# Splitting the second expert's weight quarters at other tiles of a retention and mixture-of-experts kernel

## The chip, the cores and the metric

The kernel runs on one core of one Trainium2 chip. The metric is the device time of one execution in microseconds (us). Three executions of the kernel before were timed; their median is 397.33 us (395.97 to 397.36).

## What is computed

A retention layer (linear attention with a decay per head) gives 3072 rows of 512 numbers. Each row then goes through one of 8 experts, two matrix products with a ReLU between them, and is scaled by its gate weight.

```python
# q, k, v: (4, 8, 768, 64); w_gate (512, 8); w1 (8, 512, 1024); w2 (8, 1024, 512)
for t in range(S):
    state = gamma * state + einsum('bhd,bhe->bhde', k[:, :, t], v[:, :, t])
    y[:, :, t] = scale * einsum('bhd,bhde->bhe', q[:, :, t], state)
x = y.transpose(0, 2, 1, 3).reshape(B * S, H * D)
logits = x @ w_gate
expert_idx = argmax(logits, axis=1)
gate_w = softmax(logits)[arange(N), expert_idx]
for e in range(E):
    mask = expert_idx == e
    out[mask] = gate_w[mask, None] * (maximum(x[mask] @ w1[e], 0) @ w2[e])
```

## The kernel before

The first part (to some 117 us of the span) computes the retention, the gates and the place of each row, and scatters the rows into a region of device memory for each expert. The second part, `moe_main`, goes through the experts in the order e = 0 to 7, one after the other; the change lies in it alone. Expert 0's rows come in two groups. The first group's first layer runs at the end of the first part, so that `moe_main` begins with the second group: 224 rows, from 121.5 us on.

**Precision.** Every matrix product is made of three: each operand is split into a high part (a rounded copy) and a low part (the rest), and TensorE multiplies high by high, low by high and high by low. So every weight and every activation passes through a split: a copy on ScalarE (ACT) that makes the high part, then a subtraction on VectorE (DVE) that makes the low part.

**Weights.** An expert's weights are four quarters of 1 MB. Quarters 0 and 1 belong to the first layer (tiles 0 to 3 and 4 to 7), quarters 2 and 3 to the second. "Quarter 2/0" below is quarter 0 of expert 2. `fetch` (L139) is a DMA from SyncE's queue (SP) into one of two buffers, `raw`; so a quarter's fetch waits until the quarter two before it in the order of fetches has been split. `split` (L142) splits one half of a quarter: an ACT copy (L147, `whi<-raw`) and a DVE subtraction (L148, `wlo<-raw,whi`).

**An expert's steps.** The first layer has 8 tiles f (`for f in range(KF)`). In each, TensorE makes 12 matmuls into one of three PSUM tiles `ph` (L959), ACT the ReLU `hh` (L971), and DVE the low part `hl` (L973); TensorE may write a `ph` again when the `hl` of three tiles before has been made. The second layer has steps k: four of 24 matmuls for experts 1 to 6 (L1000), two for expert 0 (L998; its third step is behind a count that leaves it out here). A step's 24 matmuls take `hh` and `hl` of tile 0 first and of tile 7 last. The results lie in two PSUM tiles `py` in turn; DVE takes them out with `yo` (L886, expert 0) or a transposition `Z` (L896), and step k + 2 needs that `py` free.

**Rows of the next expert.** `fetch_x` clears 96 rows behind the region (L702, from `zero`) and then loads the rows with four DMAs on SP (L186, `xgs<-xs_dram`); the loads wait until the clearing has landed. `prep_x` prepares up to 128 rows: a DVE transposition (L736, `xt`), an ACT copy (L745, `xh`) and the low part (L746, `xl`, on DVE or GpSimd). The first matmul of the next expert needs `xh` of all its pieces.

**What sets the order.** The order on each engine is the order of the code. `job(f, fn, ...)` files a call into a list for place f; places 0 to 7 stand behind the ReLU and low part of tile f, place `KF + k` behind step k. In each place the calls run in the order in which they were filed. Every engine takes its instructions strictly in that order, and SP its DMAs.

Of the kernel before, what the change touches and what calls it, by code (L numbers as in the profile page):

```python
# [37 lines left out]
KF = F // P  # L38
# [74 lines left out]
def retention_moe(ctx, tc, qkv, wts, cst, gdec, out):  # L113
# [587 lines left out]
    def clear_behind(e, zero):  # L701
        nc.sync.dma_start(out=x_rows[bass.ds(end_at[e], ZROWS), :], in_=zero)  # L702

    natural = {0: (sidx0, meta0)}
    moe_main(tc, wparts, fetch, split, xhl1, hidden_early, third, lim, xgs, clear_behind, load_x, load_meta, token_index, regions, beyond, limit, spare, natural,
             overflow, out)
    most = nc.values_load(top[0:1, 0:1], min_val=0, max_val=N)  # L707
# [93 lines left out]
def moe_main(ctx, tc, wparts, fetch, split, xhl1, hidden_early, third, lim, xgs, clear_behind, load_x, load_meta, token_index, regions, beyond, limit, spare, natural,  # L801
             overflow, out):
    nc = tc.nc
    sidx0, meta0 = natural[0]
# [101 lines left out]
    with tc.manual_schedule():  # L906
        for e in range(E):
# [9 lines left out]
            job = lambda f, fn, *a: jobs[f].append((fn, a))  # L917
            if e == 0:
                job(2, nc.gpsimd.memset, zero, 0.0)
                job(3, nc.vector.memset, rare[0:widths[0][2]], 0.0)  # L920
                job(4, token_index, sidx0[:, 1:4], meta0[:, 1:4], lim[:, 1:4], "joint")
                for i in range(3):
                    job(1 + i // 2, nc.vector.memset, phs[i][:, CAPS[1] - 3 * STEPS[1]:], 0.0)
                for j in range(nxt):
                    job(6 + j // 2, prep_x, 1, j, nc.vector if j % 2 else nc.gpsimd)
            if e == 1:
                job(1, put_rows, 0, rare, 2)
                job(3, overflow)
# [5 lines left out]
                job(0, fetch_x, e + 1)  # L934
            if e > 0:
                for i, eng in halves:
                    job(i, split, e, 3, i, eng)
            if back:
                nb = blocks[e - 1]
                for j in range(nb):  # L940
# [1 line left out]
                    job(at, weigh, e - 1, j, 1)  # L942
                    job(at, put_slices, e - 1, j)
            if more:
                for part, s0, f0 in ((0, 3, 0), (1, 6, 2)) if e else ((0, 2, 4), (1, 5, 7)):
                    job(f0, fetch, e + 1, part if e else part + 2)
                    for i, eng in halves:
                        job(s0 + i, split, e + 1, part, i, eng)
                if e:
                    job(6, fetch, e + 1, 2)  # L950
# [27 lines left out]
            for k in range(steps):  # L978
# [40 lines left out]
                    turn(e, py, k)  # L1019
                if more and k < 2:  # L1020
                    for i, eng in halves:
                        if i == k:
                            split(e + 1, 2, i, eng)
                if more and e and k == 0:
                    fetch(e + 1, 3)
# [143 lines left out]
```

## Time and profile before

| | before |
|---|---|
| median of three executions | 397.33 us |
| the profiled execution, device time | 395.59 us |
| its span, first to last instruction | 393.6 us |
| TensorE busy | 380.0 us, 97% |
| VectorE busy | 258.0 us, 66% |
| ScalarE busy | 154.3 us, 39% |
| GpSimd busy | 163.1 us, 41% |
| granted TensorE clock, mean | 0.995 |

The span is one profiled execution; the device time lies 2.0 us above it. Since TensorE is busy nearly throughout, what counts is where it stands still, and what it waits for there. A time in the trace is counted in us from the span's start.

### The profile page before, as it was taken

What the parts mean: (1) busy time and instruction counts of PE and PEld (TensorE: products, weight loads), DVE (VectorE), ACT (ScalarE), POOL (GpSimd) and SP (SyncE); (2) the same over time, 40 slices, a digit from 0 to 9 for tenths busy, and PEclk for the clock granted to TensorE, in tenths of its full rate; (3) what the DMA queues carried; (4) which work ended last, traced back from release to release, by engine and by line L of the source; (5) the groups of instructions that cost most, each with busy time, mean ns of one, the idle gap of its engine ahead of it and who ended that gap; (6) DMA issues with size and microseconds to landing.
All of it is one profiled execution on the core that took longest, in us unless ns stands there. A gap on an engine that the chain in (4) does not pass through costs nothing. (4 is left out here: it accounts for less than half of the span.)

```text
span 393.6 us, 8661 instructions
## 1 busy us (share of the span) xinstructions
PE 380.0 (97%) x3255; PEld 353.6 (90%) x3255; DVE 258.0 (66%) x563; ACT 154.3 (39%) x316; POOL 163.1 (41%) x153
## 2 busy tenths in 40 slices
PE   7999999998899989999999999999999999999994
PEld 4888888896799869999999999999999999999973
DVE  4547758786586787774785677477747857776330
ACT  2335444551473534633442354054334515523100
POOL 0322656846551032000653174328316614831652
PEclk9999999999899999999999999999999999999999
DMA  7998799995457659483568175835754783530111
GB/s 273 415 380 335 287 414 422 402 359 184 142 193 205 155 169 301 151 205 122 149 239 194 52 245 171 210 113 158 210 151 147 259 209 103 188 120 11 55 29 69
DMA packets 30190, 80.65 MB, mean 205 GB/s; under 512 B 4795, under 2 KB 18751, under 8 KB 23716
## 3 DMA queue, kind: packets, MB, share of 16 engines
q1 hardware_dynamic: 24868, 66.87, 52.6%
q0 software_dynamic: 5248, 12.69, 9.0%
q8 instruction: 58, 0.95, 1.0%
q14 instruction: 16, 0.13, 0.1%
HBM read 65.07 MB, written 15.19 MB: 204 GB/s over the span
## 5 line engine op out<-in xcount | busy, mean ns | idle before, releaser
L726 POOL DMA_INDIRECT out<-Z,sidx x82 | 93.9, 1145 | 134.1 <-DVE Z L901 107.8
L148 DVE TENSOR_TENSOR wlo<-raw,whi 128x1024 fp32r<-128x1024 f32 (+1 forms) x67 | 75.6, 1131 | 11.0 <-ACT whi L147 9.4
L147 ACT CAST whi<-raw 128x1024 fp32r<-128x1024 f32 (+1 forms) x72 | 67.6, 952 | 5.8 <-PE ph L959 2.9
L971 ACT ACTIVATE hh<-ph 128x64 fp32r<-128x64 f32 (+7 forms) x72 | 32.3, 460 | 90.6 <-PE ph L959 79.5
L1000 PE MATMUL py<-hl,whi 128*128 128x392 f32 (+4 forms) x192 | 66.1, 344 | 0.0
L1000 PE MATMUL py<-hh,whi 128*128 128x392 f32 (+4 forms) x192 | 66.1, 344 | 0.0
L1000 PE MATMUL py<-hh,wlo 128*128 128x392 f32 (+4 forms) x192 | 66.0, 344 | 0.0
L973 DVE SCALAR_TENSOR_TENSOR hl<-ph,hh 128x64 fp32r<-128x64 f32 (+7 forms) x72 | 36.4, 515 | 35.7 <-ACT hh L971 33.5
L959 PE MATMUL ph<-xh,whi 128*128 128x392 f32 (+5 forms) x224 | 49.3, 342 | 0.0
L959 PE MATMUL ph<-xh,wlo 128*128 128x392 f32 (+5 forms) x224 | 49.0, 340 | 0.0
L959 PE MATMUL ph<-xl,whi 128*128 128x392 f32 (+5 forms) x224 | 48.9, 340 | 0.0
L959 PEld LDWEIGHTS ph<-xh,whi 128*128 128x128 f32 x224 | 40.3, 188 | 0.5
L959 PEld LDWEIGHTS ph<-xh,wlo 128*128 128x128 f32 x224 | 40.4, 188 | 0.2
L959 PEld LDWEIGHTS ph<-xl,whi 128*128 128x128 f32 x224 | 40.2, 188 | 0.2
L745 ACT CAST xh<-xt 128x512 fp32r<-128x512 f32 (+7 forms) x27 | 14.8, 552 | 58.5 <-DVE xt L736 58.5
L1000 PEld LDWEIGHTS py<-hl,whi 128*128 128x128 f32 x192 | 36.2, 188 | 0.3
L1000 PEld LDWEIGHTS py<-hh,wlo 128*128 128x128 f32 x192 | 36.1, 188 | 0.2
L1000 PEld LDWEIGHTS py<-hh,whi 128*128 128x128 f32 x192 | 36.1, 188 | 0.2
L248 POOL TENSOR_TENSOR vs<-qkv_t,cs 128x512 f32<-128x512 f32 x19 | 19.8, 1044 | 36.1 <-DMA qkv_t<-qkv 34.2
L262 DVE TENSOR_TENSOR Sb<-sp,xgs 128x512 f32<-128x512 f32 x48 | 29.9, 682 | 7.4 <-PE sp L259 4.8
L726 POOL DMA_INDIRECT xs_dram<-xn,KEY x24 | 25.2, 1052 | 16.6 <-issue 5.3
L278 ACT ACTIVATE ub<-U,cs 128x64 f32<-128x64 f32 x80 | 18.5, 314 | 28.6 <-PE U L273 25.6
(161 smaller groups left out, 519.7 us busy)
## 6 DMA issues: line engine op xcount, KB each, us to landing
raw<-w SPq DMA_DIRECT2D x32, 1024.0 KB
qkv_t<-qkv SPq DMA_DIRECT2D x18, 1024.0 KB
qkv_t<-qkv SPq DMA_DIRECT2D x4, 768.0 KB
xgs<-xs_dram SPq DMA_DIRECT2D x12, 211.2 KB
qkv_t<-qkv SPq DMA_DIRECT2D x4, 512.0 KB
xgs<-xs_dram SPq DMA_DIRECT2D x8, 227.5 KB
out<-Z,sidx POOLq DMA_INDIRECT x82
xs_dram<-zero SPq DMA_DIRECT2D x6, 195.0 KB
```

The source lines that it names most:

```text
L147: nc.scalar.copy(out=hi[:, h], in_=raw[:, h])
L148: engine.tensor_tensor(out=lo[:, h], in0=raw[:, h], in1=hi[:, h].bitcast(F32), op=ALU.subtract)
L248: engine.tensor_tensor(out=vs, in0=qs[g][:, 2].rearrange("a (h d) -> a h d", d=D), in1=cv[:, c, :].unsqueeze(2).broadcast_to([P, H, D]), o ...
L262: nc.vector.tensor_tensor(out=Sb[:, r], in0=sps[r], in1=M[:, r], op=ALU.mult)
L278: nc.scalar.activation(out=ubs[g % 3][:, p], in_=U[:, p], func=AF.Copy, scale=k_("ratio")[:, at:at + 1])
L726: sc = tc.nc.gpsimd.indirect_dma_start(out=out, out_offset=bass.IndirectOffsetOnAxis(ap=index, axis=0), in_=rows, in_offset=None, bounds_c ...
L745: nc.scalar.copy(out=xh[:, :, sl], in_=src)
L959: nc.tensor.matmul(out=ph[:, :w], lhsT=wparts[e, f // 4][a][:, kd, fo:fo + P], rhs=x[:, kd, :w], start=(n == 0), stop=(n == 3 * KD - 1))
L971: nc.scalar.activation(out=to, in_=of, func=AF.Relu)
L973: nc.vector.scalar_tensor_tensor(out=low, in0=of, scalar=0.0, in1=to.bitcast(F32), op0=ALU.max, op1=ALU.subtract)
L1000: nc.tensor.matmul(out=py[:, :cols], lhsT=a[:, f % 4, k * P:(k + 1) * P], rhs=x[:, :cols], **se)
```

## The change

Four edits in the tables of jobs of `moe_main`; nothing is added to or taken from the computation.

- Quarter 1/0 is split in expert 0's tiles 3 and 4 (tiles 2 and 3 before). Quarter 1/1 is split in the places of the second layer's steps 0 and 1 (tiles 5 and 6 before). Quarter 1/2 is split in expert 1's tiles 0 and 1 (steps 0 and 1 of expert 0 before), quarter 1/3 in its tiles 2 and 3 (tiles 0 and 1 before).
- In expert 1, quarter 2/0 is split in tiles 5 and 6 (3 and 4 before) and quarter 2/1 in the places of steps 0 and 1 (tiles 6 and 7 before), behind quarter 2/2, which stays there. From expert 2 on nothing moves.
- The pieces of expert 1's rows are prepared in tiles 6, 6, 7 and step 0 (6, 6, 7, 7 before).
- The token index of expert 0 is made one tile earlier.

```diff
-                job(4, token_index, sidx0[:, 1:4], meta0[:, 1:4], lim[:, 1:4], "joint")
+                job(3, token_index, sidx0[:, 1:4], meta0[:, 1:4], lim[:, 1:4], "joint")
...
-                    job(6 + j // 2, prep_x, 1, j, nc.vector if j % 2 else nc.gpsimd)
+                    job((6, 6, 7, KF)[j], prep_x, 1, j, nc.vector if j % 2 else nc.gpsimd)
...
                 for i, eng in halves:
-                    job(i, split, e, 3, i, eng)
+                    if e == 1:
+                        job(i, split, e, 2, i, eng)
+                    job(i + 2 * (e == 1), split, e, 3, i, eng)
...
-                for part, s0, f0 in ((0, 3, 0), (1, 6, 2)) if e else ((0, 2, 4), (1, 5, 7)):
+                for part, s0, f0 in ((0, 3 + 2 * (e == 1), 0), (1, 6 + 2 * (e == 1), 2)) if e else ((0, 3, 4), (1, KF, 7)):
                     job(f0, fetch, e + 1, part if e else part + 2)
                     for i, eng in halves:
                         job(s0 + i, split, e + 1, part, i, eng)
...
                     for i, eng in halves:
-                        if i == k:
+                        if e and i == k:
                             split(e + 1, 2, i, eng)
```

In the rows below, `wlo` is the low part of a half quarter, and its `raw` buffer tells the quarter.

VectorE in expert 0, before, from tile 5's split to tile 6 (`raw_1873` is quarter 1/1):

```order
L148 TENSOR_TENSOR wlo_2303<-raw_1873,whi_2302 128x1024
L973 SCALAR_TENSOR_TENSOR hl0_1660<-ph0_2147,hh0_1659 128x64
L973 SCALAR_TENSOR_TENSOR hl_2319<-ph0_2147,hh_2318 128x160
L736 STREAM_TRANSPOSE xt_2326<-xgs_71 128x4x4x32
L736 STREAM_TRANSPOSE xt_2330<-xgs_71 128x4x4x32
L746 TENSOR_TENSOR xl_2325<-xt_2330,xh_2324 128x4x128
```

and now, from tile 6 to step 0:

```order
L975 SCALAR_TENSOR_TENSOR hl0_1660<-ph0_2147,hh0_1659 128x64
L975 SCALAR_TENSOR_TENSOR hl_2315<-ph0_2147,hh_2314 128x160
L736 STREAM_TRANSPOSE xt_2322<-xgs_71 128x4x4x32
L736 STREAM_TRANSPOSE xt_2326<-xgs_71 128x4x4x32
L746 TENSOR_TENSOR xl_2321<-xt_2326,xh_2320 128x4x128
L975 SCALAR_TENSOR_TENSOR hl0_1660<-ph1_2148,hh0_1659 128x64
L975 SCALAR_TENSOR_TENSOR hl_2343<-ph1_2148,hh_2342 128x160
L736 STREAM_TRANSPOSE xt_2348<-xgs_71 128x4x4x32
L886 TENSOR_SCALAR yo_2378<-py0_2144,meta0_84 128x4x4x32
L736 STREAM_TRANSPOSE xt_2383<-xgs_71 128x2x4x32
L746 TENSOR_TENSOR xl_2321<-xt_2383,xh_2320 128x4x56
L148 TENSOR_TENSOR wlo_2388<-raw_1873,whi_2387 128x1024
```

Quarter 1/1 has moved from ahead of tile 6 to behind the take-out of step 0 (`yo`), and the last piece of the rows with it.

SP's queue around the end of expert 0, before (`raw_2282` and `raw_2362` are quarters 1/2 and 1/3, the branches of L1005 and L842 mark the last step of expert 0 and the first tile of expert 1):

```order
L139 DMA raw_2282<-w 128x2048
L139 DMA raw_2362<-w 128x2048
L702 ISA
L702 DMA xs_dram_61<-zero_2154 96x520
L1005 UNCONDITIONAL_BRANCH
L842 UNCONDITIONAL_BRANCH x3
```

and now (`raw_2280` and `raw_2352`):

```order
L139 DMA raw_2280<-w 128x2048
L1007 UNCONDITIONAL_BRANCH
L842 UNCONDITIONAL_BRANCH x3
L139 DMA raw_2352<-w 128x2048
L842 UNCONDITIONAL_BRANCH
L702 ISA
L702 DMA xs_dram_61<-zero_2154 96x520
```

The order of the DMAs is the same; the fetch of quarter 1/3 now waits for a split that stands at the very end of expert 0, and the clearing and expert 2's row loads stand behind it.

VectorE in expert 1, steps 0 and 1, before (`raw_2888` is quarter 2/2):

```order
L736 STREAM_TRANSPOSE xt_2949<-xgs_71 128x4x4x32
L746 TENSOR_TENSOR xl_2948<-xt_2949,xh_2947 128x4x128
L896 STREAM_TRANSPOSE Z_3052<-py0_2144 128x14x32
L148 TENSOR_TENSOR wlo_3055<-raw_2888,whi_3054 128x1024
L842 UNCONDITIONAL_BRANCH
L736 STREAM_TRANSPOSE xt_3060<-xgs_71 128x4x4x32
L746 TENSOR_TENSOR xl_2948<-xt_3060,xh_2947 128x4x128
L896 STREAM_TRANSPOSE Z_3052<-py1_2145 128x14x32
```

and now (`raw_2884` is quarter 2/2, `raw_2638` quarter 2/1):

```order
L736 STREAM_TRANSPOSE xt_2943<-xgs_71 128x4x4x32
L842 UNCONDITIONAL_BRANCH x2
L746 TENSOR_TENSOR xl_2942<-xt_2943,xh_2941 128x4x128
L896 STREAM_TRANSPOSE Z_3046<-py0_2144 128x14x32
L148 TENSOR_TENSOR wlo_3049<-raw_2884,whi_3048 128x1024
L842 UNCONDITIONAL_BRANCH
L148 TENSOR_TENSOR wlo_3055<-raw_2638,whi_3054 128x1024
L736 STREAM_TRANSPOSE xt_3058<-xgs_71 128x4x4x32
L746 TENSOR_TENSOR xl_2942<-xt_3058,xh_2941 128x4x128
L896 STREAM_TRANSPOSE Z_3046<-py1_2145 128x14x32
```

Between the take-outs of steps 0 and 1 there are now two low parts instead of one.

## Rows read from the trace of the kernel before

**Rows 1.** The page, engines: busy us (share of the span) and instructions.

```profile
PE 380.0 (97%) x3255; PEld 353.6 (90%) x3255; DVE 258.0 (66%) x563; ACT 154.3 (39%) x316; POOL 163.1 (41%) x153
```

**Rows 2.** Timeline, TensorE: start, duration, instruction, count [idle before and its releaser].

```profile
131.60 0.70 PE L959 MATMUL ph<-xhl,whi 128*128 128x224 f32 x4 [0.35 <-DVE hl L973]
...
133.04 0.41 PE L998 MATMUL py<-whi,hh 128*128 128x512 f32 x1
...
137.59 0.39 PE L998 MATMUL py<-whi,hl 128*128 128x512 f32 x1
138.45 0.50 PE L998 MATMUL py<-whi,hh 128*128 128x512 f32 x1 [0.48 <-ACT hh L971]
...
140.00 0.50 PE L998 MATMUL py<-whi,hl 128*128 128x512 f32 x1 [0.81 <-DVE hl L973]
...
145.97 0.93 PE L959 MATMUL ph<-xh,whi 128*128 128x392 f32 x4
...
163.08 0.34 PE L1000 MATMUL py<-hh,whi 128*128 128x392 f32 x1
...
180.25 0.92 PE L959 MATMUL ph<-xh,whi 128*128 128x422 f32 x4
```

**Rows 3.** Timeline, ScalarE.

```profile
132.79 1.05 ACT L147 CAST whi<-raw 128x1024 fp32r<-128x1024 f32 x1 [2.42 <-PE ph L959]
...
138.19 0.41 ACT L971 ACTIVATE hh<-ph 128x64 fp32r<-128x64 f32 x2
...
157.68 1.05 ACT L147 CAST whi<-raw 128x1024 fp32r<-128x1024 f32 x1 [2.39 <-DMA raw<-w]
...
167.37 1.05 ACT L147 CAST whi<-raw 128x1024 fp32r<-128x1024 f32 x1
...
177.30 0.42 ACT L745 CAST xh<-xt 128x272 fp32r<-128x272 f32 x1 [2.40 <-DVE xt L736]
```

**Rows 4.** Timeline, VectorE.

```profile
146.78 1.22 DVE L148 TENSOR_TENSOR wlo<-raw,whi 128x1024 fp32r<-128x1024 f32 x1
...
161.56 1.13 DVE L973 SCALAR_TENSOR_TENSOR hl<-ph,hh 128x440 fp32r<-128x440 f32 x2
...
168.50 1.19 DVE L148 TENSOR_TENSOR wlo<-raw,whi 128x1024 fp32r<-128x1024 f32 x1
...
171.00 0.69 DVE L746 TENSOR_TENSOR xl<-xt,xh 128x512 fp32r<-128x512 f32 x1 [0.69 <-ACT xh L745]
...
176.16 0.65 DVE L896 STREAM_TRANSPOSE Z<-py 128x448 f32<-128x448 f32 x1 [0.53 <-PE py L1000]
```

**Rows 5.** Timeline, SP: the issue of DMAs (the duration is that of issuing).

```profile
133.85 0.35 SPq L139 DMA_DIRECT2D raw<-w  x1
139.83 0.35 SPq L139 DMA_DIRECT2D raw<-w  x1
...
145.95 2.00 SPq L186 DMA_DIRECT2D xgs<-xs_dram  x4
...
153.54 0.35 SPq L139 DMA_DIRECT2D raw<-w  x1
161.67 0.34 SPq L139 DMA_DIRECT2D raw<-w  x1
166.04 0.33 SPq L139 DMA_DIRECT2D raw<-w  x1
...
171.95 1.90 SPq L186 DMA_DIRECT2D xgs<-xs_dram  x4
```

**Rows 6.** Stretches: length, busy of each engine, granted clock, DMA share, GB/s.

```profile
134.75:138.25 3.50, 3.23 (x15) 2.34 (x13) 2.81 (x6) 2.13 (x4) 1.29 (x1) 1.00 0.86 302
172.75:178.25 5.50, 5.50 (x32) 5.50 (x32) 3.75 (x6) 1.04 (x2) 0.00 (x0) 1.00 1.14 198
178.25:180.75 2.50, 2.50 (x16) 2.49 (x15) 0.30 (x1) 0.00 (x0) 0.00 (x0) 1.00 0.90 357
180.75:182.00 1.25, 1.25 (x9) 1.22 (x8) 0.34 (x1) 0.00 (x0) 0.00 (x0) 1.00 0.04 7
```

## The prediction

> **What bounds the kernel now.** First the page: TensorE is busy for 380.0 us of the span and VectorE for 66% of it [rows 1], so a change of order can only win where TensorE stands still, and lose where it makes it stand still. Then TensorE's own timeline through experts 0 and 1, where everything moved lies. The reader is to see three gaps in expert 0 and none in expert 1 [rows 2]. Tile 7 waits 0.35 us for the `hl` of tile 4. Step 0 waits 0.48 us for the `hh` of tile 7 and 0.81 us for its `hl`. ScalarE's timeline shows why: the copy of quarter 1/1 waited 2.42 us until 132.79 for TensorE, and the ReLU of tile 7 came only at 138.19 [rows 3], four microseconds after step 0 had begun at 133.04. It stood behind the late copy, the ReLU of tile 6, two pieces of rows and a second copy.
>
> From 145.97 (expert 1's first tile) to 163.08 (its second layer) and 180.25 (expert 2) TensorE has no wait [rows 2]. The one wait there is ScalarE's: it stood 2.39 us until quarter 2/0 had landed at 157.68 [rows 3]. That quarter is behind expert 2's row loads in SP's queue. This stretch is full, and the change puts more into it.
>
> **Part 1: expert 0.** Twenty matmuls of step 0 take 133.04 to 137.59, 0.2275 us each [rows 2]. Two steps of 24 would take 10.9 us and the short third step 0.1; from 133.04 to 145.97 it took 12.93. So 1.9 us are lost in the steps, and some 0.4 at tile 7: 2.3 us. With the change no split stands between tile 4 and step 0. Tile 7's ReLU stands behind the copies of two row pieces, which start after tile 6 and two transpositions of some 0.7 us, and so is done near 135, 2 us before step 0 needs it. The last piece of rows comes after the take-out of step 0, some 4 us before expert 1's first tile. The token index (four small operations of a tile earlier) lies beside matmuls; its cover is the wait for the ReLU, and without it the index would cost its own 0.6 us at most. The fetch of quarter 1/2 stands behind value loads in SP and goes out at 133.85 either way [rows 5]. I count the whole gap as gone: **-2.3 us**, expert 1 begins at 143.7. Its bounds are 0 and -2.3, since no more is lost there.
>
> **Part 2: when quarter 2/0 lands.** Quarter 1/3 may be fetched when quarter 1/1 is split. The second half of that split now stands behind the take-out of step 1. In the profile the same place on VectorE held a half that began at 146.78 and took 1.22 [rows 4], so ended 2.0 us after expert 1's first matmul: now 145.7, where the fetch went out at 139.83 before. Behind it in SP stand the clearing and expert 2's row loads. From such a fetch to the row loads it took 6.1 us in one place (139.83 to 145.95) and 5.9 in the other (166.04 to 171.95) [rows 5]. So the row loads go at 151.7, and quarter 2/0 behind them.
>
> How long after the loads it lands has two rows. Expert 3's loads began at 171.95 with one quarter behind them. The engines moved 198 GB/s until 178.25, then 357 (the quarter), and were quiet after 180.75 [rows 6]: 8.8 us. Expert 2's loads began at 145.95 and quarter 2/0 was there at 157.68 [rows 3, 5], 11.7 us, with quarter 2/1 issued behind it at 153.54. The new case is the same quarter, with its follower 3 us closer. Neither row fits in every respect, so I take the middle, 10.25: it lands at **161.9** (160.5 to 163.4).
>
> The Trainium skill (DMA: Bandwidth & Descriptors, Queues, rings and completion order) says that an engine takes the descriptors of one issuing engine's ring in order. By that alone the quarter would land right behind the loads, at 160.5, and the sum below would be +0.9 instead of +2.2. The rate of 198 and then 357 GB/s agrees with the order; the 11.7 us do not agree with a landing right behind. The same section says that a completion comes only when the last of the DMA engines has reported, which leaves room for them.
>
> **Part 3: what waits for it in expert 1.** Expert 1's second layer begins 17.1 us after its first tile [rows 2], now at 160.8. ScalarE's queue is now: copy of 2/0, ReLU of tile 6, copy, ReLU of tile 7; VectorE's follows in the same manner. In the profile the same sequence, two tiles earlier, ran from the landing at 157.68 to the `hl` that started at 161.56 [rows 3, 4]; the first of its two ended about 4.4 us after the landing. So the `hl` of tile 7 is ready at 166.3. Step 0 reaches it with its last matmul, 23 x 0.179 us (17.17 us for 96 matmuls, from 163.08 to 180.25 [rows 2]) after its start: 164.9. **TensorE waits 1.4 us** (0 to 2.9). Before, the same lateness stood at tiles 3 and 4, where three `ph` tiles hid it.
>
> Quarter 2/2 takes the buffer of 2/0. Its fetch went out 4.0 us after the landing (161.67 after 157.68 [rows 3, 5]): 165.9. Landing takes 4.4 us when nothing is ahead (issued at 133.85, moved by 138.25 [rows 5, 6]) and at most 5.7 (161.67 to its copy at 167.37 [rows 3, 5]). I take 4.7, near the lower row since that one is free of other waits: 170.6. From there VectorE's queue decides: copy 1.05, `wlo` of 2/2, `wlo` of 2/1 (1.15 each at their pitch), a row piece, and only then the `Z` of step 1, on which step 3 waits for its `py`. From a `wlo` at 168.50 to the end of the next `xl` (171.00 and 0.69) it took 3.2 us [rows 4]. So `Z` of step 1 ends at 170.6 + 1.1 + 1.15 + 3.2 + 0.65 = 176.7. Step 3 would begin at 160.8 + 1.4 + 3 x 4.29 = 175.1. **TensorE waits 1.6 us.** Then two more low parts, a row piece (1.15 + 3.2) and `Z` of step 2 and the last piece (176.16 to 177.30 + 0.42 [rows 3, 4], 1.6 us) must pass, 5.8 with their overlaps, before the first matmul of expert 2 has its `xh`: 182.5. Step 3 ends at 181.0. **TensorE waits 1.5 us.** In the profile that place had no wait and expert 2 began at 180.25.
>
> The three waits make 4.5 us, less the 2.3: **+2.2 us**. The ends are landings at 160.5 with 4.4 and at 163.4 with 5.7: expert 2 at 180.8 or at 185.0, +0.5 or +4.8.
>
> **Part 4: behind.** Quarter 2/3 is fetched when 2/1 is split, some 2.3 us after that `Z`, at 179.0; expert 3's loads follow 6.0 us later and quarter 3/0 lands at 193.8 to 196.7. A tile of expert 2 takes 2.14 x 422 / 392 = 2.30 us, so its tile 7 begins at 198.6 and needs an `hl` that ends some 2.8 us after the landing, at 196.6 to 199.5. I take 0; at most 0.9. From there on the orders are the same, and a delay stays a delay. The moves of 1/2 and 1/3 into tiles 0 to 3 put one half per tile of 2.14 us on ScalarE (1.05) and VectorE (1.22), beside ReLU and `hl`; `hl` may come three tiles late, so I cost it at nothing.
>
> **Sum.** 393.6 + 2.2 = 395.8 of span, 397.8 with the 2.0 around it; the profiled execution lies 1.74 below the median. On the median: 397.33 + 2.2 = **399.5 us**.
>
> **Rivals.**
> A. Slower by more: quarter 2/0 lands as the nearest row has it, 11.7 us after the loads, and expert 2 still meets a late 3/0. 163.4 + 4.0 + 4.7 + 11.9 puts expert 2 at 184.0, +3.75, and 0.5 in its tile 7: 401.6 us. For it: the very same quarter took that long. Against: 8.8 elsewhere.
> B. Faster: the quarter does not wait for the row loads to move but shares the engines with them and lands 4.4 us after an issue near 153.9, at 158.3. Then neither tile 7 nor step 3 is late by much, expert 2 begins at 178.9 and the time is 396.0; with a landing by 157.2 all of the 2.3 stays, 395.0. It decides at a landing of 159.6, from which on expert 2 is late against 180.25. Against: the 198 GB/s while the loads move, half of what a quarter reaches [rows 6].
> C. The change doesn't do what it says in expert 0: the ReLU of tile 7 is late still, now behind the row copies. Then 1 us of step 0's gap, say, remains, and parts 2 and 3, whose times all count from the end of expert 0, come on top of it: 400.5. Against: a margin of 2 us.
>
> **How the numbers follow.** A measurement of this kernel can tell about 0.5%, 2.0 us, from no change. My forecast has a chance of 0.65; its own range is +0.5 to +3.4, and I put 0.34 above 2.0 us and 0.31 below. A has 0.16, all slower. B has 0.12: 0.07 faster by over 0.5%, 0.05 within. C has 0.04, slower. The remaining 0.03 lies within. Slower 0.54, same 0.39, faster 0.07. The range of 8 in 10 runs from 397.2 to 402.0: it leaves out B and the far end of A.
>
> **What would show it.** After the change: no wait of TensorE for `hh` or `hl` in expert 0 and expert 1's first matmul near 143.7 (part 1). The row loads near 151.7 and a wait of ScalarE for quarter 2/0 until about 162 (part 2). Waits of TensorE at the end of step 0, before step 3 and before expert 2's first matmul, for `hl`, `Z` and `xh` (part 3). If quarter 2/0 is there before 159.6, I am wrong in sign; if the three waits are there but expert 2 begins before 181, only the size is off.

## The result, and the profile after

| | kernel before | kernel after |
|---|---|---|
| median of the runs made side by side, us | 396.69 (395.97 to 397.36, 4 runs) | 401.87 (401.38 to 402.15, 4 runs) |
| span of the profiled execution, us | 393.6 | 400.0 |
| first tile of expert 0 behind the early half, us | 121.55 | 121.68 |
| expert 1 begins | 145.97 | 143.73 |
| copy of quarter 2/0 begins on ScalarE | 157.68 | 165.43 |
| expert 2 begins | 180.25 | 186.18 |
| expert 3 begins | 217.25 | 223.31 |

The ratio is 1.0129 with an interval of [1.0103, 1.0156]: the kernel after is 1.3% slower, 5.2 us. The forecast was 399.5 us, 2.2 us more than before; its range of 397.2 to 402.0 holds the time, near the upper end. That is partly luck: the kernel before came out at 396.69 this time and not at the 397.33 of the forecast, and 5.2 us on top of 397.33 would have been 402.5, outside the range.

On the page, the busy time of TensorE has grown by 4.5 us though no matmul was added, which is the first hint of a slower clock [rows 1]:

```profile
PE 384.5 (96%) x3255; PEld 355.3 (89%) x3255; DVE 258.0 (64%) x563; ACT 154.3 (39%) x316; POOL 163.0 (41%) x153
```

TensorE's timeline after (start, duration, instruction, count, idle before and its releaser), to be laid beside [rows 2]:

```profile
121.68 0.68 PE L961 MATMUL ph<-xhl,whi 128*128 128x224 f32 x4 [0.97 <-DVE xhl L680]
...
143.73 0.57 PE L961 MATMUL ph<-xh,whi 128*128 128x392 f32 x2
...
160.85 0.34 PE L1002 MATMUL py<-hh,whi 128*128 128x392 f32 x1
...
166.97 0.70 PE L1002 MATMUL py<-hh,whi 128*128 128x392 f32 x1 [2.73 <-ACT hh L973]
...
168.31 0.69 PE L1002 MATMUL py<-hl,whi 128*128 128x392 f32 x1 [0.33 <-DVE hl L975]
...
169.97 0.70 PE L1002 MATMUL py<-hl,whi 128*128 128x392 f32 x1 [0.31 <-DVE hl L975]
...
186.18 1.04 PE L961 MATMUL ph<-xh,whi 128*128 128x422 f32 x4 [1.05 <-ACT xh L745]
...
223.31 0.91 PE L961 MATMUL ph<-xh,whi 128*128 128x418 f32 x4
```

The reader sees two things. The gap in expert 0 is gone: from its first tile to expert 1 it is 22.05 us where it was 24.42. And expert 1, which had no wait before, now has four. From its first matmul to expert 2 it takes 42.45 us, where it took 34.28. Behind that nothing changes: from expert 2 to expert 3 it is 37.13 us after and 37.00 before.

SP's timeline after (the duration is that of issuing), against [rows 5]: quarter 1/3, the clearing, expert 2's row loads, then quarters 2/0 and 2/1 together, and 2/2.

```profile
145.78 0.35 SPq L139 DMA_DIRECT2D raw<-w  x1
146.47 0.37 SPq L702 DMA_DIRECT2D xs_dram<-zero  x1
154.15 2.94 SPq L186 DMA_DIRECT2D xgs<-xs_dram  x4
157.34 0.95 SPq L139 DMA_DIRECT2D raw<-w  x2
169.42 0.34 SPq L139 DMA_DIRECT2D raw<-w  x1
```

ScalarE's and VectorE's timelines after, against [rows 3, 4]: the copies of quarters 2/0 and 2/2, and VectorE's chain from the late quarter to the last row piece of expert 2.

```profile
165.43 1.04 ACT L147 CAST whi<-raw 128x1024 fp32r<-128x1024 f32 x1 [8.11 <-DMA raw<-w]
174.41 2.00 ACT L147 CAST whi<-raw 128x1024 fp32r<-128x1024 f32 x2 [3.22 <-DMA raw<-w]
```

```profile
166.51 1.22 DVE L148 TENSOR_TENSOR wlo<-raw,whi 128x1024 fp32r<-128x1024 f32 x1 [8.54 <-ACT whi L147]
167.65 0.61 DVE L975 SCALAR_TENSOR_TENSOR hl<-ph,hh 128x440 fp32r<-128x440 f32 x1
168.18 1.21 DVE L148 TENSOR_TENSOR wlo<-raw,whi 128x1024 fp32r<-128x1024 f32 x1
169.31 0.61 DVE L975 SCALAR_TENSOR_TENSOR hl<-ph,hh 128x440 fp32r<-128x440 f32 x1
...
175.49 2.36 DVE L148 TENSOR_TENSOR wlo<-raw,whi 128x1024 fp32r<-128x1024 f32 x2 [3.02 <-ACT whi L147]
...
179.77 0.64 DVE L896 STREAM_TRANSPOSE Z<-py 128x448 f32<-128x448 f32 x1
180.34 2.32 DVE L148 TENSOR_TENSOR wlo<-raw,whi 128x1024 fp32r<-128x1024 f32 x2
...
186.16 0.44 DVE L746 TENSOR_TENSOR xl<-xt,xh 128x272 fp32r<-128x272 f32 x1 [0.48 <-ACT xh L745]
```

From the copy at 165.43 every step of VectorE follows the one before it or the next landing, down to the last row piece, beside which expert 2 starts. Call the start of that copy **L**: expert 2 begins at L + 20.75.

The stretches of core 0 after show where the wait's second effect lies (length, busy time of PE, PEld, DVE, ACT and POOL, granted clock, DMA share, GB/s):

```profile
152.00:154.00 2.00, 2.00 (x13) 2.00 (x12) 1.47 (x5) 2.00 (x3) 0.03 (x1) 1.00 0.04 6
157.00:162.00 5.00, 5.00 (x30) 5.00 (x29) 0.85 (x2) 0.32 (x1) 0.00 (x0) 1.00 1.20 222
162.00:165.40 3.40, 2.23 (x13) 1.91 (x11) 0.00 (x0) 0.00 (x0) 0.00 (x0) 1.00 1.00 412
167.00:173.00 6.00, 5.33 (x13) 3.88 (x14) 4.79 (x7) 1.91 (x3) 0.00 (x0) 0.50 0.42 138
173.00:186.00 13.00, 12.12 (x67) 11.79 (x65) 8.81 (x11) 5.44 (x7) 0.00 (x0) 0.98 0.31 102
```

Behind the wait of 2.73 us the granted clock is 0.50, the 1.2 GHz level, until about 173.5; matmuls of 392 columns then follow each other at 0.33 us instead of 0.18. From 160.85 the 17.17 us of work in expert 1's second layer [rows 2] and the 3.37 us of waits would end at 181.4, and TensorE is done at 185.1, 3.7 us later. The half clock is at most 3.4 us of that, half of the 6.8 us that it lasts; what the rest is, the rows do not tell.

The first of these stretches is the second thing that was not foreseen. The row loads wait for the clearing, which landed only at 154.15, 7.7 us after its issue, though the engines moved almost nothing from 152 on.

### The profile page after: what moved, and what is told of

Read it like the earlier page. It is cut to its first block, busy times and chain, and to the rows that moved or that the text cites. A ratio compares the mean times of both kernels' runs of the same rounds, so it can differ in the third digit from the quotient of the medians.

```text
span 400.0 us, 8666 instructions
## 1 busy us (share of the span) xinstructions
PE 384.5 (96%) x3255; PEld 355.3 (89%) x3255; DVE 258.0 (64%) x563; ACT 154.3 (39%) x316; POOL 163.0 (41%) x153
## 5 line engine op out<-in xcount | busy, mean ns | idle before, releaser
L148 DVE TENSOR_TENSOR wlo<-raw,whi 128x1024 fp32r<-128x1024 f32 (+1 forms) x67 | 77.1, 1155 | 21.1 <-ACT whi L147 20.0
L1002 PE MATMUL py<-hh,whi 128*128 128x392 f32 (+4 forms) x192 | 67.3, 351 | 2.8 <-ACT hh L973 2.7
L1002 PE MATMUL py<-hl,whi 128*128 128x392 f32 (+4 forms) x192 | 67.3, 350 | 0.6 <-DVE hl L975 0.6
L1002 PE MATMUL py<-hh,wlo 128*128 128x392 f32 (+4 forms) x192 | 67.0, 349 | 0.0
L248 POOL TENSOR_TENSOR vs<-qkv_t,cs 128x512 f32<-128x512 f32 x19 | 19.9, 1047 | 35.8 <-DMA qkv_t<-qkv 35.5
```

The lines of the kernel that those rows point to most:

```text
L148: engine.tensor_tensor(out=lo[:, h], in0=raw[:, h], in1=hi[:, h].bitcast(F32), op=ALU.subtract)
L248: engine.tensor_tensor(out=vs, in0=qs[g][:, 2].rearrange("a (h d) -> a h d", d=D), in1=cv[:, c, :].unsqueeze(2).broadcast_to([P, H, D]), o ...
L1002: nc.tensor.matmul(out=py[:, :cols], lhsT=a[:, f % 4, k * P:(k + 1) * P], rhs=x[:, :cols], **se)
```

## The experiments

**The theory at the start:** the whole loss comes from the landing of quarter 2/0. Its chain is fixed, so expert 2 starts at L + 20.7 whatever is done around it, and L is late because quarter 1/3, the clearing, the row loads and 2/0 stand in one queue behind the late split of quarter 1/1. **The rivals:** the order of splits in expert 1 costs by itself; the slow clock costs by itself; the rows' new places cost.

**1. Both halves of quarter 1/1 behind step 0 of expert 0, nothing else undone** (half11_early). In the kernel after, the second half stands behind step 1, the last full step.

```diff
-                        job(s0 + i, split, e + 1, part, i, eng)
+                        job(s0 + i * (e > 0 or part == 0), split, e + 1, part, i, eng)
```

> The changed kernel, but the second half of quarter 1/1 is split in the place of step 0 too, not step 1. If the landing of quarter 2/0 sets everything (theory): quarter 1/3 is fetched at 143.2 instead of 145.8, row loads at 149 to 152, quarter 2/0 lands 2.5 to 5 us earlier (160.5 to 163), expert 2 begins 20.7 us after that, at 181 to 184, time 2.5 to 5 us below the changed kernel (397 to 399.5). If it is the two low parts between the take-outs whatever the landing (rival): within 1 us of the changed kernel, 401 to 402.

Measured: 397.04 us, ratio to before 1.0005 [0.9977, 1.0033], so 4.8 us under the kernel after. Three rows of its timelines: the loads, the copy of 2/0 and expert 2's start.

```profile
148.83 1.96 SPq L186 DMA_DIRECT2D xgs<-xs_dram  x4
```

```profile
159.77 1.05 ACT L147 CAST whi<-raw 128x1024 fp32r<-128x1024 f32 x1 [3.08 <-DMA raw<-w]
```

```profile
180.54 1.03 PE L961 MATMUL ph<-xh,whi 128*128 128x422 f32 x4 [1.15 <-ACT xh L745]
```

Expert 2 starts 20.77 us behind the copy, as in the kernel after, while the copy is 5.7 us earlier. One half of one split, moved by a step, takes back 4.8 of the 5.2 us of loss: it decides when quarter 1/3 may be fetched (142.56 here, 145.78 after) and with it all that stands behind it in SP's queue. But not all of this is the fetch. Counted from expert 1's first tile (143.10 here), the copy is 5.0 us earlier than after: the fetch of 1/3 gives 2.6 of them, and 2.1 come from the clearing, which took 5.6 us here instead of 7.7.

**2. Expert 0's last group of rows taken out and scattered in tile 6 of expert 1, not in tile 1** (rare_late), to see whether this scatter, which ran beside the clearing, made the clearing late.

```diff
-                job(1, put_rows, 0, rare, 2)
+                job(6, put_rows, 0, rare, 2)
```

> The changed kernel, but expert 0's third group of rows is taken out and scattered in tile 6 of expert 1, not tile 1. If the scatter at 150.4 held back the landing of the clearing (landed at 154.1, 7.7 us after its issue, 5.2 in the kernel before): row loads at 151.8 instead of 154.15, quarter 2/0 some 2.4 us earlier, time 399.5. If the clearing is late for another reason: row loads at 154 as in the changed kernel, 401.9 +- 0.5.

Measured: 402.52 us, ratio 1.0149 [1.0109, 1.0188]. The clearing still took 7.6 us (145.21 to the loads at 152.78) without that scatter beside it. That idea of mine fell. The take-out of the rows (0.73 us on VectorE) now stands in the chain, and expert 2 starts at L + 21.33, 0.6 later than elsewhere: the chain is so tight that what is put into it shows in full.

**3. Clearing and row loads of expert 2 behind the fetch of quarter 2/0** (loads_behind).

```diff
-            if more and e:
+            if more and e > 1:
                 job(0, fetch_x, e + 1)
...
+                if e == 1:
+                    job(0, fetch_x, e + 1)
```

(The second piece stands behind the fetch of quarter 2/0.)

> The changed kernel, but the clearing and expert 2's row loads stand behind the fetch of quarter 2/0 in SP's queue. Theory: quarter 2/0 is issued at 151.4 and lands near 156, ScalarE doesn't wait for it, TensorE has no wait in step 0 and keeps its clock; the row loads now delay quarter 2/2, so some 0.5 to 1 us of wait stays before step 3; expert 2 begins at 179.5 to 181, time 396 to 397.5. Rival (two low parts between the take-outs cost as much by themselves): 400 or more.

Measured: 398.51 us, ratio 1.0055 [1.0028, 1.0082], between the 396 to 397.5 of the theory and the 400 of the rival. ScalarE no longer waits for quarter 2/0 at all, and TensorE does not wait for `hh` or `hl`. But now the loads go out at 159.41, quarters 2/1 and 2/2 at 162.68, and 2/2 lands at 172.76; TensorE's timeline shows the wait at the next place of the chain, the `Z` of step 1:

```profile
178.81 0.70 PE L1004 MATMUL py<-hh,whi 128*128 128x392 f32 x1 [3.37 <-DVE Z L896]
```

In this profiled execution expert 2 starts 41.9 us behind expert 1, barely less than after (42.45), while the median of ten runs is 3.4 us under that of after; so this one profile does not account for the median, and only the place of the new wait is taken from it.

**4. The first part of the change alone** (gap_only): quarter 1/0 and the token index moved as in the kernel after and both halves of 1/1 put behind tile 7; quarter 2/0 is split in expert 1's tiles 4 and 5, one tile later than before, and quarters 1/2, 1/3 and 2/1 where the kernel before has them.

```diff
-                job(4, token_index, sidx0[:, 1:4], meta0[:, 1:4], lim[:, 1:4], "joint")
+                job(3, token_index, sidx0[:, 1:4], meta0[:, 1:4], lim[:, 1:4], "joint")
...
-                for part, s0, f0 in ((0, 3 + (e == 1), 0), (1, 6, 2)) if e else ((0, 2, 4), (1, 5, 7)):
+                for part, s0, f0 in ((0, 3 + (e == 1), 0), (1, 6, 2)) if e else ((0, 3, 4), (1, 7, 7)):
...
-                        job(s0 + i, split, e + 1, part, i, eng)
+                        job(s0 + i * (e > 0 or part == 0), split, e + 1, part, i, eng)
```

(This diff is against the kernel before; the rows' places are those of before.)

> The kernel before with the gap of expert 0 alone attacked: quarter 1/0 in tiles 3 and 4, token index a tile earlier, both halves of quarter 1/1 behind tile 7 after the rows, quarters 1/2 and 1/3 as before; in expert 1 quarter 2/0 one tile later (4 and 5), 2/1 as before (6 and 7). Theory: expert 1 begins at 143.7 (2.3 earlier); quarter 1/3 is fetched at 141.5, row loads at 147.5 to 149, quarter 2/0 lands at 156.5 to 160; no wait of TensorE longer than 1 us in expert 1; time 394.5 to 396, 1 to 2.3 below the kernel before. Rival (any delay of quarter 1/1 costs what the gap gives): 396.5 to 398.

Measured: 396.12 us, ratio 1.0003 [0.9975, 1.003], between the 394.5 to 396 of the theory and the 396.5 to 398 of the rival. In the profile the gap is gone (22.06 us from expert 0's first tile to expert 1), and most of it is given back ahead of expert 2, which begins 18.88 us behind the second layer instead of 17.17. ScalarE's row for the copy of 2/0 says why:

```profile
159.02 1.05 ACT L147 CAST whi<-raw 128x1024 fp32r<-128x1024 f32 x1 [4.63 <-DMA raw<-w]
```

The work runs 2.4 us earlier, the quarter does not. Up to expert 2 this leaves 0.65 us of gain. In the same profile TensorE also stands 1.94 us in the middle of a step of expert 2; the profile names a low part of expert 3's weights as the releaser, which that matmul doesn't read. Behind that wait the granted clock is 0.50 for 3.4 us. The kernel before has the same rows on ScalarE and VectorE around that place and no such wait. What it is stays open.

**5. The clearing ahead of the fetch of quarter 1/3** (clear_early), everything else as in the kernel after.

```diff
+            if e == 0:
+                job(6, clear_behind, 2, zero)
...
     def fetch_x(e):
-        clear_behind(e, zero)
+        if e != 2:
+            clear_behind(e, zero)
```

> The kernel after, with one change: the clearing of the rows behind expert 2's is issued during expert 0, ahead of the fetch of quarter 1/3, instead of behind it; the four row loads stand where they were and then wait for nothing but their turn. Theory (the cause is that quarter 2/0 lands late because the row loads ahead of it wait 7.7 us for the clearing): the loads go out right behind the fetch of 1/3, near 146.5 us instead of 154.15, the fetch of 2/0 some 3 us later near 149.7, and its copy starts 11.3 us after the loads, near 158 instead of 165.43. Then expert 2 cannot start before the copy + 20.75 = 179, where the work alone allows 178.0, against 186.18 in the kernel after: 6 to 7 us less, a median of 395 to 396. Rival (the order of the splits itself, with both low parts between other work on VectorE, costs the time wherever the quarter lands): the copy comes early but expert 2 still starts 2 to 4 us late, median 398 to 400. Second rival (the buffer, not the loads, holds quarter 2/0): the copy moves by less than 3 us, median 399 or more.

Measured: 397.89 us, ratio 1.0039 [1.0019, 1.0059], 4.0 us under the kernel after: less than the 6 to 7 expected, and just under the 398 to 400 of the first rival, whose mechanism did not come, since expert 2 starts no later behind the copy. The rows of SP, ScalarE and TensorE:

```profile
147.05 0.35 SPq L139 DMA_DIRECT2D raw<-w  x1
147.66 3.36 SPq L186 DMA_DIRECT2D xgs<-xs_dram  x4
...
152.57 0.35 SPq L139 DMA_DIRECT2D raw<-w  x1
```

```profile
162.62 1.05 ACT L147 CAST whi<-raw 128x1024 fp32r<-128x1024 f32 x1 [4.04 <-DMA raw<-w]
```

```profile
183.24 1.03 PE L964 MATMUL ph<-xh,whi 128*128 128x422 f32 x4 [1.15 <-ACT xh L745]
```

The loads go right behind quarter 1/3, as expected. But L comes 15.0 us behind them instead of 11.3: the data of 1/3 and of the loads share the engines, and 2/0 itself goes out only at 152.57, when a low part of quarter 1/2 frees its buffer. Counted from expert 0's first tile (122.94 here), L is 4.1 us earlier than after and expert 2 4.2 us, at L + 20.62. So the clearing was 4 us of the loss and the rest of the 6 to 7 us went to the next limits in the queue, the transfers and the buffer.

**6. Twelve extra matmuls in TensorE's wait** (clock_filled), to keep its clock up.

```diff
+DUMMY = 12
...
-    rare = ps_between.tile([P, 2, DM], F32, name="between")[:, 0]
+    rare = ps_between.tile([P, 2, DM], F32, name="between")
+    rare, spin = rare[:, 0], rare[:, 1, 0:392]
...
+                        if e == 1 and k == 0 and f == 6:
+                            for _ in range(DUMMY):
+                                nc.tensor.matmul(out=spin, lhsT=whi[:, f % 4, 0:P], rhs=hs[0][0][:, :392], start=True, stop=True)
```

> The kernel after, with twelve extra matmuls of 392 columns, into a half of a PSUM tile that nothing reads, issued in step 0 of expert 1 just ahead of tile 6's products, so that TensorE works through part of its 2.73 us wait there. It asks what the fall of the granted clock to 0.50 after that wait costs. Theory (the chain through the late quarter on ScalarE and VectorE sets the start of expert 2, and the slow products lie beside it): the granted clock stays up between 167 and 173 us, the steps 0 and 1 are done some 3 us earlier, a wait ahead of step 3 takes the place, and the median stays at 401 to 402.5. Rival (the slow clock is itself part of the loss): 2 to 3 us less, a median of 399 to 400. If the clock falls all the same, the run tells nothing.

Measured: 402.41 us, ratio 1.0148 [1.0117, 1.0179], no change against after. The clock fell all the same, only later, as its stretches show:

```profile
166.00:169.00 3.00, 1.43 (x5) 0.78 (x5) 3.00 (x5) 1.44 (x3) 0.00 (x0) 1.00 0.01 3
169.00:173.00 4.00, 3.67 (x11) 3.41 (x12) 1.95 (x4) 0.63 (x1) 0.00 (x0) 0.60 0.76 266
```

So this run does not answer by itself. Experiments 1 and 5 do: there the granted clock was 1.00 from L to expert 2, and the chain took the same 20.6 to 20.8 us.

**7. Quarter 2/1 back in tiles 6 and 7, 2/0 as after** (second_back).

```diff
-                for part, s0, f0 in ((0, 3 + 2 * (e == 1), 0), (1, 6 + 2 * (e == 1), 2)) if e else ((0, 3, 4), (1, KF, 7)):
+                for part, s0, f0 in ((0, 3 + 2 * (e == 1), 0), (1, 6, 2)) if e else ((0, 3, 4), (1, KF, 7)):
```

> The kernel after, with the halves of quarter 2/1 split in tiles 6 and 7 of expert 1, where the kernel before has them, and quarter 2/0 in tiles 5 and 6 as after. It asks what the move of the second quarter to steps 0 and 1 costs by itself, with the first quarter as late as it is. Theory (copy of 2/0 + 20.75 us is the start of expert 2 because the low parts of 2/1 stand between the results of the steps on VectorE): the copy of 2/0 starts within 1 us of 165.4, the wait of step 0 for hl grows by about 1 to 2.5 us, the work after it is shorter, and expert 2 starts some 18 to 19.5 us behind the copy, 1 to 2.5 us less in all, a median of 399.5 to 401. Rival (all that counts is when 2/0 lands): 401 to 402.5, no change.

Measured: 401.25 us, ratio 1.0124 [1.0093, 1.0154]. L is 163.80 (21.2 us behind expert 1, 21.7 after), and VectorE's chain got shorter as expected: its last row piece starts at L + 19.55. Yet expert 2 starts at L + 22.04. The row of VectorE, then the stretch and the start of expert 2 on TensorE:

```profile
183.35 0.44 DVE L746 TENSOR_TENSOR xl<-xt,xh 128x272 fp32r<-128x272 f32 x1 [0.49 <-ACT xh L745]
```

```profile
166.00:176.00 10.00, 8.19 (x22) 6.86 (x23) 8.27 (x11) 4.57 (x7) 0.00 (x0) 0.50 0.66 231
176.00:185.80 9.80, 9.80 (x56) 9.80 (x55) 5.32 (x8) 2.34 (x4) 0.00 (x0) 1.00 0.85 204
```

```profile
185.84 0.92 PE L961 MATMUL ph<-xh,whi 128*128 128x422 f32 x4
```

TensorE waits longer in step 0 (2.21, 0.72, 0.42 and 0.65 us), runs at half its clock from 166 to 176, and now comes last: the slow clock, hidden in the kernel after, takes the gain here. The half clock lasts 10.2 us and so costs up to 5.1; without it TensorE would have been done before VectorE's last row piece at 183.35, by this estimate, which no run tests. Neither theory had that.

**8. gap_only with loads_behind** (gap_and_behind); the diff is against gap_only.

```diff
-            if more and e:
+            if more and e > 1:
                 job(0, fetch_x, e + 1)
...
+                if e == 1:
+                    job(0, fetch_x, e + 1)
```

> The kernel that does the change's first part alone (gap_only: the gap ahead of expert 1 closed, quarters 2/0 and 2/1 split where the kernel before has them), and with the clearing and the row loads of expert 2 behind the fetch of quarter 2/0, as in loads_behind. Theory (the order of the queue ahead of 2/0 is what is left): quarter 2/0 is there when its copy's turn comes, the wait of 4.63 us on ScalarE goes, expert 2 starts 17.2 us behind the second layer of expert 1 instead of 18.9, and the median is 394 to 395.2, under both kernels. Rival (quarter 2/1 or the rows then come late): the wait moves to the copy of 2/1 or to the first tiles of expert 2, and the median is 396 to 398.

Measured: 402.47 us (399.22 to 405.86), ratio 1.014 [1.0099, 1.0182]: the rival, and worse than it said. The profiled execution is the longest of the six, so only the place of the wait is taken from its rows. (Quarter 2/0 is split in tiles 4 and 5 here too, as in gap_only.) Quarter 2/0 has no wait, but the clearing, issued at 146.78, held the loads until 155.66, and the quarter behind them, 2/1, is what comes late:

```profile
166.75 1.04 ACT L147 CAST whi<-raw 128x1024 fp32r<-128x1024 f32 x1 [7.08 <-DMA raw<-w]
```

**9. and 10. The early clearing added to experiments 1 and 4** (early_both, gap_clear_early). The edit is that of experiment 5 on those two kernels; in the second the clearing goes into tile 5:

```diff
+            if e == 0:
+                job(5, clear_behind, 2, zero)
...
     def fetch_x(e):
-        clear_behind(e, zero)
+        if e != 2:
+            clear_behind(e, zero)
```

> half11_early (both halves of quarter 1/1 split in the last step of expert 0, everything else as in the kernel after) together with the early clearing of clear_early: the clearing behind expert 2's rows goes out ahead of the fetch of quarter 1/3. In half11_early quarter 1/3 went out at 142.55 us, the clearing at 143.24, the loads at 148.83, the fetch of 2/0 near 151, and its copy waited 3.08 us until 159.77; expert 2 began 20.77 us behind that copy. In clear_early the copy began 15.0 us behind the loads, because the data of 1/3, the loads and 2/0 then shared the engines. Theory (expert 2 begins 20.6 to 20.8 us behind the copy of 2/0 or, if later, when the products alone allow, 34.3 us behind expert 1): loads near 143.3, copy some 15 us later near 158, expert 2 near 178.8, 1.7 us less than half11_early: a median of 395 to 396. Rival (the bandwidth over 1/3, loads and 2/0 is what is short, and the order among them gives nothing): the copy near 159.8 again, a median of 396.5 to 397.5. Seen the other way: if the copy comes by 156.7 expert 2 starts as the products allow, near 177.5, and the median is 394.

Measured: 395.61 us, ratio to before 0.9953 [0.9934, 0.9973]. The copy of 2/0 comes at 159.32, 14.25 us behind expert 1's first tile (16.67 in experiment 1), and expert 2 at L + 20.78. The time is the theory's.

> gap_only (the gap ahead of expert 1 closed, quarters 2/0 and 2/1 split where the kernel before has them) together with the clearing behind expert 2's rows ahead of the fetch of quarter 1/3. In gap_only the clearing went out at 141.52 us, the loads at 147.31, the fetches of 2/0 and 2/1 at 150.58, and the copy of 2/0 waited 4.63 us until 159.02; expert 2 began 19.9 us behind it, 36.0 behind expert 1, where the products alone take 34.3. Theory: the loads go out near 142.3, the copy near 157, and the wait of 1.7 us ahead of expert 2 shrinks to under 0.3: a median of 394.3 to 395.3, under both kernels. Rival (bandwidth, as above): the copy near 159 and a median of 396 to 396.5.

Measured: 394.48 us, ratio 0.9941 [0.9912, 0.9969]: as the theory had it, and faster than both kernels. TensorE's timeline in it shows the gap closed and nothing put in its place:

```profile
122.24 0.67 PE L962 MATMUL ph<-xhl,whi 128*128 128x224 f32 x4 [0.63 <-DVE xhl L680]
...
144.30 0.93 PE L962 MATMUL ph<-xh,whi 128*128 128x392 f32 x4
...
161.41 0.34 PE L1003 MATMUL py<-hh,whi 128*128 128x392 f32 x1
...
178.57 0.92 PE L962 MATMUL ph<-xh,whi 128*128 128x422 f32 x4
```

From expert 0's first tile to expert 1 it is 22.06 us and from there to expert 2 34.27, the lengths of the products themselves; together 56.33 us, where the kernel before took 58.70 and the kernel after 64.50. ScalarE still waits 1.47 us for quarter 2/0, at 157.22, which three `ph` tiles cover.

The chain in one table (times in us; the last column tells whether a stretch between L and expert 2 has the granted clock under 1.00):

| kernel | L | last `xl` starts | expert 2 begins | expert 2 − L | granted clock under 1.00 |
|---|---|---|---|---|---|
| after | 165.43 | 186.16 | 186.18 | 20.75 | yes |
| clock_filled | 164.58 | 185.26 | 185.28 | 20.70 | yes |
| clear_early | 162.62 | 183.22 | 183.24 | 20.62 | no |
| half11_early | 159.77 | 180.52 | 180.54 | 20.77 | no |
| early_both | 159.32 | 180.08 | 180.10 | 20.78 | no |
| rare_late (one take-out more in the chain) | 163.82 | 185.13 | 185.15 | 21.33 | yes |
| second_back (2/1 out of the chain) | 163.80 | 183.35 | 185.84 | 22.04 | yes |

Of the rivals, the slow clock costs nothing in the kernel after, as the last column shows. The rows' new places cost nothing that can be seen: from expert 0's first tile to expert 1 it is 22.05 us in the kernel after and 22.06 in gap_only, which has the old places. The order of splits in expert 1 is a small part: gap_only, with nearly the old order, begins expert 2 19.9 us behind the copy of 2/0 instead of 20.7, and from expert 0's first tile to expert 2 early_both takes 57.06 us where gap_clear_early takes 56.33.

## Why the prediction was right in sign and too small

**Part 1 was right.** The gap was counted as 2.3 us and fully gone; 2.37 us went. gap_clear_early shows that it is real gain: its profile keeps the 2.37 us up to expert 3, and its median is lower.

**Part 2 is the term that was mis-sized.** The fetch of quarter 1/3 came when it was forecast (145.78 for 145.7). The landing of 2/0 did not: 161.9 was forecast, 18.2 us behind expert 1's first tile, and it was 165.43, 21.7 behind it. Two steps of it failed. The row loads were to follow 6.0 us behind the fetch of 1/3, from two places that agreed; here it took 8.4, since the clearing needed 7.7 us. And from the loads to the landing it took 11.3 us, where I took the middle of 8.8 and 11.7; the nearest row, the same quarter in the kernel before, had said 11.7, and rival A was built on it. In the five us from 157 the engines moved 222 GB/s, and the quarters came at 412 GB/s from 162 on. From 157 to 165.4 that makes some 2.5 MB, more than the rest of the loads and one quarter: 2/1 had moved too, most of it.

The same is to be seen in the kernel before, where 2/1 went out 7.6 us behind the loads [rows 5] and not 3.8 as here. These are the rows of SP's queue (packets, megabytes, share) from the loads to the copy of 2/0 in the kernel before (145.95 to 157.68) and after (154.15 to 165.43), and from expert 3's loads until the engines were quiet in the kernel before (171.95 to 180.75).

```profile
q1 hardware_dynamic: 2229, 2.87, 94.1%
...
q1 hardware_dynamic: 2228, 2.87, 99.3%
...
q1 hardware_dynamic: 1990, 1.96, 96.2%
```

Four loads and one quarter are 1.98 MB; that is all that the third row holds, since no second quarter followed there. In the first two the copy came when most of the follower, 0.9 of its 1.05 MB, had moved as well. It is so in seven kernels (these two, half11_early, rare_late, gap_only, clock_filled and second_back): 2.83 to 2.95 MB by the copy, which came 10.9 to 11.7 us behind the loads, with 2/1 issued anywhere from 3.4 to 7.6 us behind them. So the forecast's two rows were not two readings of one case, and the middle between them had no ground: 8.8 is the row without a follower, 11.7 the one with it, and how close the follower stands made no difference. Why the first quarter is there only with most of the second is not shown.

The Trainium skill (DMA: Bandwidth & Descriptors, Queues, rings and completion order) has an engine take one ring's descriptors in order; by that alone the landing would have been 8.8 us behind the loads, and the 11.3 us here speak against that as a time of completion. The Trainium skill (DMA: Bandwidth & Descriptors, Why a DMA increments its semaphore by 16 and not by 1) also has a completion wait for the last of the engines. The clearing below agrees: the loads went out at 154.15, behind the last of its late packets at 153.5.

The clearing's row is this one: the DMA engines of the kernel after from 152.0 to 154.1 (busy tenths and GB/s in 40 slices, then packets, megabytes and share of each queue). Quarter 1/3 had landed by then, since its copy began at 151.73, so what was left in SP's queue is the clearing.

```profile
DMA  1100000000010003000020002001000000000000
GB/s 40 40 0 0 0 0 0 0 0 0 0 1 1 1 0 40 0 0 0 0 40 0 0 0 40 0 0 40 0 0 0 0 0 0 0 0 0 0 0 0
...
q1 hardware_dynamic: 10, 0.01, 2.7%
q0 software_dynamic: 34, 0.00, 0.9%
```

Ten packets hold up the loads: the last six rows of 96, one by one, and four of 4 bytes. rare_late has the same thin tail. Its cause is not settled; it isn't the scatter moved in experiment 2. One candidate stands in the traces. In the five kernels where the last six rows needed 1.4 to 1.9 us (after, rare_late, clock_filled, second_back, gap_and_behind), a packet of 16 KB on the queue that the profile calls instruction, some 0.96 us long, began while the clearing's rows moved; in the kernel after it ran from 151.86 to 152.83, and the next row began at 152.82. In the four others (before, half11_early, gap_only, loads_behind) the six rows needed 0.1 to 0.3 us, and such a packet began beside the last row, behind it or not at all. Against it speaks expert 3's clearing in the kernel before: there such a packet began among the rows too, at 170.95, and the last six needed 0.1 us. No run moves that packet, so it stays a candidate. The thin tail is 1.3 of the 2.3 us that the clearing took longer than before.

**Part 3 had the right chain, with one wait in another form.** From the landing on, expert 2 was to start at 182.5, 20.6 us behind it; it started 20.75 behind it, and experiments 1, 5 and 9 give the same length for copies from 159.3 to 162.6. Quarter 2/2 was copied 9.0 us behind L (8.7 forecast). The `hl` of tile 7 was ready 4.5 us behind the landing (4.4 forecast). The wait in step 0 was 3.4 us in three pieces where 1.4 were forecast, which is the late landing once more. The wait of 1.6 us ahead of step 3 did not come: the steps ahead of it took 3.7 us longer, most of it the half clock, and TensorE reached step 3 at 180.7, when the `Z` of step 1 was done (179.77 and 0.64). The wait ahead of expert 2 was 1.05 us (1.5 forecast).

**Part 4 was right:** nothing more is lost in expert 2 (37.13 against 37.00 us). ScalarE waits 2.1 us there for quarter 3/0, and TensorE does not.

In sum the forecast was −2.3 + 4.5 = +2.2 us up to expert 2. The landing, 3.5 us later than forecast, goes through the chain in full, and the chain is 0.15 longer: +5.85. The profile has +5.80 (64.50 − 58.70), the medians +5.2. Rival A had the right direction of the error and the right cause for a third of it, the 11.7 us; it missed the clearing. That its 401.6 us lies so near to the 401.87 is luck: it had expert 2 at 184.0, 2.2 us too early, added 0.5 us in expert 2 that did not come, and started from the higher 397.33. Rivals B and C did not come.

## What to carry to other kernels

Closing a gap by putting work off is worth what the queue behind that work allows: here the splits that were put off closed a gap of 2.4 us and cost 8.2 us in expert 1. One half of one split, moved behind a step, held the buffer for a fetch, and with it a clearing, four loads and another fetch in the same queue; put back by a step, it gave back 5.0 of the 8.2, though 2.1 of these came with a shorter clearing. Ask of each operation that is put off which buffer it frees and who stands in line behind the fetch that waits for it. Where a transfer gates others in a queue without itself needing their place, as the clearing here, issue it ahead of the fetch that may have to wait: that alone turned the change from 1.3% slower to 0.4% slower, and with the splits of gap_only into 0.6% faster.

## What the runs showed of the hardware that was not expected

- After waits of 2.2 to 2.7 us TensorE's granted clock stood at 0.50 (1.2 GHz) for some 7 and 10 us, in the kernel after and in second_back. It costs at most 3.4 us of products in the first and nothing of the time, because VectorE's chain came last; in second_back it came last itself.
- A clearing of 195 KB took between 5.4 us (before) and 7.7 us (after) from its issue to the loads that wait for it, 8.9 us in gap_and_behind; in the kernel after the engines were almost idle in the last 2 us of it.
- Of two quarters of 1 MB behind the row loads, the first was there only when most of the second had moved: 8.1 us after its issue with the second 0.6 us behind it (after), 9.5 us with the second 5.4 us behind it (before). A quarter with nothing ahead needs some 4.4 [rows 5, 6].
